# A two-layer decode step: one more V tile kept in SBUF, a smaller ring for wo and w1, and wo in products of 512 columns

## The chip, the cores and the metric

The kernel runs on 1 core of one Trainium2 chip. The metric is the device time of one execution in microseconds (us); less is better. Times are the median of several executions, and one more execution was profiled.

## The reference

Two equal layers, with the same weights and caches, run on one token for each of 8 batches. Each layer adds attention over a cache of 4096 positions, and then a dense block:

```python
x = x + _A_ref(_layernorm(x), k_cache, v_cache, wq, wo)   # 32 query heads, 4 K/V heads of 128
x = x + _B_ref(_layernorm(x), w1, b1, w2, b2)             # gelu(x @ w1 + b1) @ w2 + b2
...
x: 8 x 1 x 1024     k, v: 8 x 4 x 4096 x 128     wq: 1024 x 4096     wo: 4096 x 1024
w1: 1024 x 3584     w2: 3584 x 1024
```

All of it is float32. One layer reads 8 MB of K and 8 MB of V for each batch, 16 MB each of wq and wo, and 14 MB each of w1 and w2, unless something is still in SBUF.

## The kernel before

**Arena.** Nearly all of SBUF is one tile, `arena`: 52 places of 0.5 MB (1024 columns of 128 partitions, `SCW`). A list written ahead of time, `stream`, names every tile that is to be loaded, its size in places and the place where it goes, in the order in which it will be used. `pump()` issues the list in order from SyncE (L244); SyncE stands at a transfer until its places have been freed, and everything behind it on the list stands too. `release()` frees a tile's places when its last product has been issued and pumps again. There is no other order of loads.

**Attention.** For each batch there are eight K tiles and eight V tiles of 1 MB, taken in transfers of 1, 2 or 4 MB (the lists in `batch(...)` give size in places and place). `scores()` (L557) multiplies K, `probs()` does the softmax, `values()` (L600) multiplies V, `heads()` (L612) folds the result into `oT`. Layer 0 takes the batches from 0 to 7, layer 1 from 7 to 0, so that tiles of batch 7's V that are still in SBUF need not be loaded again: `n_kept` of them, 7.

**wo, w1.** `project()` (L383) multiplies `oT` by wo: for each of 32 heads, four products of 256 columns, one to each quarter of the output's partitions, all added up in one PSUM tile `y`. L392 adds `y` to the residual. `layernorm()` follows, then `expand()` multiplies w1 (L273; the last group of columns in L276), and each group of 512 columns goes through `hidden()`: a scaled copy on ScalarE (L290), transposes (L356), and the gelu on DVE (L360 to L373). In layer 0, while 7 MB of kept V (places 28 to 41) and 14 MB of wq (places 0 to 27) stay where they are, wo and w1 go through a ring: places 42, 45, 48, 50, of 3, 3, 2 and 2 places, so tiles of 1.5 and 1 MB.

**w2 and the next layer's queries.** `swap()` runs between the layers. In each of eight steps it multiplies 128 columns of w2 (L421, `down`), adds the result to the transposed residual `xv` (L485), and at once multiplies that part of `xv` by its rows of wq (L319, `q_part`), in two halves: `used(k, 0)` right then, `used(k, 1)` deferred to the next step. Each half frees its places of wq, and w2's later parts go there: `W2_PARTS` and `W2_LAST` name the places. w2 stays for layer 1, where `down_row()` (L439) multiplies it in the other direction, four blocks after each group of w1. A pair of w2 blocks is one product of 256 columns where the two lie next to each other or at a distance that is a power of two, otherwise two products of 128 columns. The last rows of w2 are loaded again at the very end (`LATE`).

**Small things.** `bsel` is a matrix that adds up the four quarters of the partitions; `row_s` is a scratch row of 512 columns.

Of the kernel before, what the change touches and what calls it, by code (L numbers as in the profile page):

```python
# [8 lines left out]
F32 = mybir.dt.float32  # L9
# [34 lines left out]
W2_PARTS = (((0, 16, 42), (16, 8, 44)), ((0, 16, 46), (16, 8, 48)), ((16, 8, 49), (0, 16, 50)), ((16, 8, 45), (0, 16, 2)),  # L44
            ((0, 16, 4), (16, 8, 6)), ((0, 16, 8), (16, 8, 10)), ((16, 8, 7), (0, 16, 11)), ((0, 16, 13), (16, 8, 15)))
W2_LAST = 45, 0, 1, 0
W2_COLS = NFT * Q4
LATE_AT = 0, 1, 40, 41
# [61 lines left out]
def decode_layers(ctx: ExitStack, tc: tile.TileContext, x, kc, vc, wq, wo, w1, w2, out):  # L110
# [12 lines left out]
    bits = const.tile([P, 3 + B + 2 * HQ + REP + T + 18], F32, name="bits")  # L123
# [36 lines left out]
    idq = ident.rearrange("p (j r h) -> p j r h", j=HKV, r=4)[:, :, 0, :]  # L160

    bsel = bit(B)
    nc.vector.tensor_reduce(bsel, idq.rearrange("p j h -> p h j"), AX.X, ALU.add)
# [213 lines left out]
    def project(name, lhs, resid, rsum, hooks={}):  # L377
        y = ps_o.tile([P, CH], F32, tag="o", name="y")
        n = 0
        for slot in tiles((name,)):  # L380
            for c in range(0, slot.cols, D):
                for j in range(4):
                    nc.tensor.matmul(y[32 * j:32 * j + 32, 0:Q4], lhs[:, n * B:n * B + 32],  # L383
                                     slot.ap[:, c + j * Q4:c + (j + 1) * Q4],
                                     start=(n == 0), stop=(n == HQ - 1))
                n += 1
                if n in hooks:
                    hooks[n]()
            release(slot)
            flush()  # L390
        assert n == HQ
        nc.vector.scalar_tensor_tensor(resid, y[:, 0:Q4], 1.0, resid, op0=ALU.mult, op1=ALU.add, accum_out=rsum)  # L392
# [54 lines left out]
    def swap():  # L447
# [15 lines left out]
        for s in range(NT):  # L463
# [23 lines left out]
            if k < NT - 1:  # L487
                used(k, 0)
                late.append(lambda k=k: used(k, 1))
# [223 lines left out]
    n_kept = 7  # L713
# [25 lines left out]
    batch(0, last_b, ((8, 28), (4, 36), (4, 40)), ((2, 48), (8, 28), (4, 36), (2, 40)))  # L739
    weights(("o0",), wo[0], [3, 3, 2, 2] * 3 + [2], fixed(*(42, 45, 48, 50) * 3, 42))  # L740
    weights(("i0",), w1[0], [1, 3, 2, 2] + [3, 3, 2, 2] * 2, fixed(44, 45, 48, 50, *(42, 45, 48, 50) * 2))
# [8 lines left out]
    batch(1, last_b, ((2, 16), (4, 20), (4, 24), (2, 18), (2, 0), (2, 16)), ((2, 20),))  # L750
    batch(1, last_b - 1, ((4, 24), (2, 22), (4, 16), (2, 0), (4, 36)), ((8, 28), (8, 16)))
# [129 lines left out]
```

## Time and profile before

| | us |
|---|---|
| median of 3 runs | 851.18 (850.93 to 853.94) |
| profiled execution | 850.72 |
| its span, first to last instruction | 848.9 |
| TensorE (PE) busy | 527.5 |
| VectorE (DVE) busy | 203.3 |
| ScalarE (ACT) busy | 56.4 |
| HBM read | 357.78 MB |

The span is what the profile's views count in; 1.8 us of the execution lie around it. Times in the views are us from the span's start. The layers' parts lie about so: queries of layer 0 until 48, attention until 361, wo until 398, w1 until 433, swap until 477, attention of layer 1 until 775, wo until 806, w1 and w2 until 846.

### The profile page before, as it was taken

What the parts mean: (1) busy time and instruction counts of PE and PEld (TensorE: products, weight loads), DVE (VectorE), ACT (ScalarE), POOL (GpSimd) and SP (SyncE); (2) the same over time, 40 slices, a digit from 0 to 9 for tenths busy, and PEclk for the clock granted to TensorE, in tenths of its full rate; (3) what the DMA queues carried; (4) which work ended last, traced back from release to release, by engine and by line L of the source; (5) the groups of instructions that cost most, each with busy time, mean ns of one, the idle gap of its engine ahead of it and who ended that gap; (6) DMA issues with size and microseconds to landing.
All of it is one profiled execution on the core that took longest, in us unless ns stands there. A gap on an engine that the chain in (4) does not pass through costs nothing.

```text
span 848.9 us, 9798 instructions
## 1 busy us (share of the span) xinstructions
PE 527.5 (62%) x4234; PEld 178.4 (21%) x4234; DVE 203.3 (24%) x698; ACT 56.4 (7%) x120; POOL 2.2 (0%) x13
## 2 busy tenths in 40 slices
PE   0745655566656657556778785576655666555787
PEld 0211111111111111122234222121111121112345
DVE  0013232313223131400121243141413222231022
ACT  0110000000000000000211100000000000000031
POOL 0000000000000000000000000000000000000000
PEclk9987868767787878787899988877878786888779
DMA  9999999999999999999999999999999999999997
GB/s 401 419 430 436 422 437 422 439 425 435 422 427 439 424 434 429 418 423 416 414 408 416 422 395 433 432 440 424 435 429 432 428 434 430 432 431 432 419 424 285
DMA packets 22362, 358.53 MB, mean 422 GB/s; under 512 B 2480, under 2 KB 3120, under 8 KB 5424
## 3 DMA queue, kind: packets, MB, share of 16 engines
q1 hardware_dynamic: 22176, 357.77, 99.1%
q8 instruction: 33, 0.54, 0.3%
q10 hardware_dynamic: 144, 0.15, 0.1%
q14 instruction: 9, 0.07, 0.0%
HBM read 357.78 MB, written 0.13 MB: 422 GB/s over the span
## 4 chain that ended last, share of the span: by engine, by line
DMA 73%; PE 22%; DVE 2%; issue 1%; another core or an unknown queue 1%; ACT 1%; SPq 0%; ACTq 0%; DVEq 0%
DMA arena<-in_k_dram 26%; DMA arena<-in_v_dram 22%; DMA arena<-in_w_dram 12%; PE o_ps L600 8%; DMA arena<-in_wo_dram 8%; PE sps L557 7%; DMA arena<-in_wq_dram 5%; PE y L383 1%; PE acc L273 1%; PE acc L319 1%; PE sps L421 1%; PE sps L612 1%; PE sps L590 0%; ACT sps L581 0%
## 5 line engine op out<-in xcount | busy, mean ns | idle before, releaser
L557 PE MATMUL sps<-arena,qz 128*32 128x512 f32 x1024 | 166.1, 793 | 118.3 <-DMA arena<-in_k_dram 117.8
L600 PE MATMUL o_ps<-arena 128*32 128x512 f32 x512 | 86.0, 802 | 52.4 <-DMA arena<-in_v_dram 45.5
L600 PE MATMUL o_ps<-arena,spare 128*32 128x512 f32 x512 | 81.0, 749 | 40.9 <-DMA arena<-in_v_dram 31.7
L557 PEld LDWEIGHTS sps<-arena,qz 128*32 128x32 f32 x1024 | 37.5, 135 | 211.4 <-issue 169.3
L605 DVE SCALAR_TENSOR_TENSOR scr<-o_ps,bits,scr 128x128 f32<-128x128 f32 x192 | 67.4, 351 | 6.8
L383 PE MATMUL y<-arena,oxT 128*32 128x256 f32 x512 | 42.6, 488 | 29.6 <-DMA arena<-in_wo_dram 29.6
L603 DVE TENSOR_SCALAR scr<-o_ps,bits 128x128 f32<-128x128 f32 x64 | 22.4, 351 | 144.1 <-PE o_ps L600 144.1
L273 PE MATMUL acc<-arena,oxT 128*32 128x512 f32 x192 | 33.1, 724 | 9.9 <-DMA arena<-in_w_dram 9.5
L319 PE MATMUL acc<-arena,oxT 128*32 128x512 f32 x248 | 32.4, 635 | 7.1 <-DMA arena<-in_wq_dram 4.5
L612 PEld LDWEIGHTS sps<-bits,scr 128*128 128x128 f32 x128 | 21.9, 215 | 67.4 <-issue 45.6
L600 PEld LDWEIGHTS o_ps<-arena 128*32 128x32 f32 x512 | 16.9, 133 | 85.4 <-issue 64.8
L613 DVE TENSOR_TENSOR oxT<-sps,scr 128x8 f32<-128x8 f32 x64 | 10.5, 165 | 93.4 <-PE sps L612 93.4
L562 DVE TENSOR_SCALAR_CACHE_REDUCE spare<-sps 128x512 f32<-128x512 f32 x16 | 11.1, 692 | 87.7 <-PE sps L557 87.7
L600 PEld LDWEIGHTS o_ps<-arena,spare 128*32 128x32 f32 x512 | 16.6, 126 | 69.4 <-issue 46.9
L562 DVE TENSOR_SCALAR_CACHE_REDUCE arena<-sps 128x512 f32<-128x512 f32 x16 | 11.1, 692 | 83.4 <-PE sps L557 83.4
L581 ACT ACTIVATE sps<-arena,bits 128x512 f32<-128x512 f32 x16 | 10.9, 682 | 284.2 <-DVE scr L575 284.2
L383 PEld LDWEIGHTS y<-arena,oxT 128*32 128x32 f32 x512 | 18.1, 135 | 52.3 <-DMA arena<-in_wo_dram 33.8
L581 ACT ACTIVATE sps<-spare,bits 128x512 f32<-128x512 f32 x16 | 10.9, 682 | 267.1 <-DVE scr L575 267.1
L612 PE MATMUL sps<-bits,scr 128*128 128x8 f32 x128 | 27.8, 290 | 0.0
L571 PE MATMUL sps<-scr,bits 128*128 128x128 f32 x32 | 7.6, 322 | 22.9 <-DVE scr L567 22.9
L421 PE MATMUL sps<-arena,oxT 128*32 128x128 f32 x448 | 16.0, 275 | 4.0 <-DMA arena<-in_w_dram 3.7
L204 PE MATMUL sps<-ident,xb 128*128 128x128 f32 x6 | 1.5, 344 | 24.3 <-DMA xb<-in_x_dram 23.2
(125 smaller groups left out, 256.2 us busy)
## 6 DMA issues: line engine op xcount, KB each, us to landing
arena<-in_v_dram SPq DMA_DIRECT2D x26, 4096.0 KB, 21.7
arena<-in_k_dram SPq DMA_DIRECT2D x21, 4096.0 KB, 21.5
arena<-in_k_dram SPq DMA_DIRECT2D x19, 2048.0 KB, 17.3
arena<-in_w_dram SPq DMA_DIRECT2D x16, 1024.0 KB, 10.4
arena<-in_v_dram SPq DMA_DIRECT2D x7, 2048.0 KB, 18.7
arena<-in_wo_dram SPq DMA_DIRECT2D x3, 4096.0 KB, 23.6
arena<-in_w_dram SPq DMA_DIRECT2D x6, 2048.0 KB, 23.1
arena<-in_wo_dram SPq DMA_DIRECT2D x6, 1536.0 KB, 10.5
```

The lines of the kernel that those rows point to most:

```text
L273: nc.tensor.matmul(acc[32 * j:32 * j + 32, :], lhs, slot.ap[:, c:c + CH], start=(kt < 4), stop=(kt >= NT - 4))
L319: nc.tensor.matmul(acc[u][32 * j:32 * j + 32, d0 - j * CH:d1 - j * CH], xnT[:, kt * XS:kt * XS + 32], ap[:, d0 - c0:d1 - c0], start=(kt == ...
L383: nc.tensor.matmul(y[32 * j:32 * j + 32, 0:Q4], lhs[:, n * B:n * B + 32], slot.ap[:, c + j * Q4:c + (j + 1) * Q4], start=(n == 0), stop=(n ...
L421: nc.tensor.matmul(y[32 * g:32 * g + 32], h_at(kt), arena.ap[:, a:a + P], start=(n < 4), stop=(n >= NFT - 4))
L557: nc.tensor.matmul(ps[32 * g:32 * g + 32, :], qz[:, c:c + 32], kt[:, g * CH:(g + 1) * CH], start=(j == 0), stop=(j == HKV - 1))
L562: nc.vector.tensor_scalar(st["row", b].ap[:, half * CH:(half + 1) * CH], ps, SCALE, None, op0=ALU.mult, op1=ALU.max, accum_out=st["mx", b] ...
L581: nc.scalar.activation(pp, row[:, h * CH:(h + 1) * CH], AF.Exp, bias=bias, scale=1.0, accum_out=ls[:, h:h + 1])
L600: nc.tensor.matmul(o[32 * g:32 * g + 32, :], s[:, g], v[:, g * CH:(g + 1) * CH], start=(half == 0), stop=(half == NH - 1))
L603: nc.vector.tensor_scalar(r, o[:, 0:P], sel_t[:, 0:1], None, op0=ALU.mult)
L605: nc.vector.scalar_tensor_tensor(r, o[:, t * P:(t + 1) * P], sel_t[:, t:t + 1], r, op0=ALU.mult, op1=ALU.add)
L612: nc.tensor.matmul(po[:, 0:REP], r_s[j % 2], sel_h, start=True, stop=True)
L613: nc.vector.tensor_tensor(oT_v[:, j * REP:(j + 1) * REP, b], po[:, 0:REP], rl_s[b % 2][:, j * REP:(j + 1) * REP], ALU.mult)
```

## The change

Seven edits go together:

- `n_kept` is 8: all of batch 7's V stays for layer 1, which loads none of it.
- The ring of layer 0's wo and w1 is four tiles of 1 MB, in places 44, 46, 48 and 50 (eight places in all).
- `W2_PARTS`, `W2_LAST` and `LATE_AT` name other places for w2; batches 7, 6 and 5 of layer 1 get other places and cuts.
- `project()` multiplies wo in two products of 512 columns for each head. Even heads go to quarters 0 and 2 of the output's partitions, odd heads to quarters 1 and 3.
- So `y` holds two halves for each column that have to be added: DVE copies one half of the partitions to `row_s`, ScalarE the other, and four products with `fold`, a matrix of 32 columns that takes the place of `bsel` and contains it, add them up.
- In `swap()`, the first step multiplies its second half of wq at once.
- `bits` grows by 24 columns for `fold`.

```diff
-W2_PARTS = (((0, 16, 42), (16, 8, 44)), ((0, 16, 46), (16, 8, 48)), ((16, 8, 49), (0, 16, 50)), ((16, 8, 45), (0, 16, 2)),
-            ((0, 16, 4), (16, 8, 6)), ((0, 16, 8), (16, 8, 10)), ((16, 8, 7), (0, 16, 11)), ((0, 16, 13), (16, 8, 15)))
-W2_LAST = 45, 0, 1, 0
+W2_PARTS = (((0, 16, 44), (16, 8, 50)), ((0, 16, 48), (16, 8, 46)), ((16, 8, 47), (0, 16, 0)), ((16, 8, 51), (0, 16, 4)),
+            ((16, 8, 3), (0, 16, 6)), ((0, 16, 10), (16, 8, 9)), ((0, 16, 12), (16, 8, 2)), ((0, 16, 14), (16, 8, 8)))
+W2_LAST = 51, 2, 8, 16
...
-LATE_AT = 0, 1, 40, 41
+LATE_AT = 40, 41, 42, 43
...
+    fold = bit(32)
+    nc.vector.tensor_reduce(fold, ident.rearrange("p (j m) -> p m j", j=4), AX.X, ALU.add)
+    bsel = fold[:, 0:B]
...
-                for j in range(4):
-                    nc.tensor.matmul(y[32 * j:32 * j + 32, 0:Q4], lhs[:, n * B:n * B + 32],
-                                     slot.ap[:, c + j * Q4:c + (j + 1) * Q4],
-                                     start=(n == 0), stop=(n == HQ - 1))
+                for h in range(2):
+                    g = 2 * h + n % 2
+                    nc.tensor.matmul(y[32 * g:32 * g + 32, :], lhs[:, n * B:n * B + 32],
+                                     slot.ap[:, c + h * CH:c + (h + 1) * CH], start=(n < 2), stop=(n >= HQ - 2))
...
-        nc.vector.scalar_tensor_tensor(resid, y[:, 0:Q4], 1.0, resid, op0=ALU.mult, op1=ALU.add, accum_out=rsum)
+        nc.vector.tensor_copy(row_s[0:P // 2], y[0:P // 2])
+        nc.scalar.activation(row_s[P // 2:P], y[P // 2:P], AF.Copy)
+        both = small_ps("s")
+        for j in range(4):
+            at = slice(j // 2 * 64, j // 2 * 64 + 64)
+            nc.tensor.matmul(both[32 * j:32 * j + 32, 0:Q4], fold[at], row_s[at, j % 2 * Q4:(j % 2 + 1) * Q4], start=True, stop=True)
+        nc.vector.scalar_tensor_tensor(resid, both[:, 0:Q4], 1.0, resid, op0=ALU.mult, op1=ALU.add, accum_out=rsum)
...
-                late.append(lambda k=k: used(k, 1))
+                if s == 0:
+                    used(k, 1)
+                else:
+                    late.append(lambda k=k: used(k, 1))
...
-    n_kept = 7
+    n_kept = 8
...
-    batch(0, last_b, ((8, 28), (4, 36), (4, 40)), ((2, 48), (8, 28), (4, 36), (2, 40)))
-    weights(("o0",), wo[0], [3, 3, 2, 2] * 3 + [2], fixed(*(42, 45, 48, 50) * 3, 42))
-    weights(("i0",), w1[0], [1, 3, 2, 2] + [3, 3, 2, 2] * 2, fixed(44, 45, 48, 50, *(42, 45, 48, 50) * 2))
+    batch(0, last_b, ((8, 28), (4, 36), (4, 40)), ((4, 28), (8, 32), (4, 40)))
+    weights(("o0",), wo[0], [2] * 16, fixed(*(48, 46, 44, 50) * 4))
+    weights(("i0",), w1[0], [2] * 14, fixed(*(48, 46, 44, 50) * 4))
...
-    batch(1, last_b, ((2, 16), (4, 20), (4, 24), (2, 18), (2, 0), (2, 16)), ((2, 20),))
-    batch(1, last_b - 1, ((4, 24), (2, 22), (4, 16), (2, 0), (4, 36)), ((8, 28), (8, 16)))
-    batch(1, last_b - 2, ((4, 36), (4, 24), (8, 28)), ((8, 16), (8, 24)))
+    batch(1, last_b, ((2, 20), (2, 22), (4, 24), (4, 16), (2, 20), (2, 22)), ())
+    batch(1, last_b - 1, ((4, 24), (4, 16), (4, 20), (4, 28)), ((8, 32), (8, 16)))
+    batch(1, last_b - 2, ((4, 24), (4, 28), (8, 32)), ((8, 16), (8, 24)))
```

What the numbers in the lists move shows in the order of the instructions. On SyncE, through wo, w1 and the first of w2, the list of transfers was this (128x2048 is 1 MB, 128x3072 1.5 MB, 128x1024 0.5 MB; `in_w_dram` is w1 and then w2):

```order
L244 DMA arena<-in_wo_dram 128x3072 x2
L244 DMA arena<-in_wo_dram 128x2048 x2
L244 DMA arena<-in_wo_dram 128x3072 x2
L244 DMA arena<-in_wo_dram 128x2048 x2
L244 DMA arena<-in_wo_dram 128x3072 x2
L244 DMA arena<-in_wo_dram 128x2048 x3
L244 DMA arena<-in_w_dram 128x1024
L244 DMA arena<-in_w_dram 128x3072
L244 DMA arena<-in_w_dram 128x2048 x2
```

The same list with the change, as far as the first part of w2 that goes into place 0 (the last row):

```order
L244 DMA arena<-in_wo_dram 128x2048 x16
L244 DMA arena<-in_w_dram 128x2048 x15
L244 DMA arena<-in_w_dram 128x1024 x2
L244 DMA arena<-in_w_dram 128x2048
L244 DMA arena<-in_w_dram 128x1024 x2
L244 DMA arena<-in_w_dram 128x2048
```

wo's 13 transfers are 16 equal ones; the row of 15 is w1's 14 and the first of w2, and 4 MB of w2 stand ahead of the part for place 0.

On TensorE, at the end of layer 1 before the change, wo (L383) goes over into the layer norm, w1 (L273) and the first group of w2 (L439):

```order
L383 MATMUL y<-arena,oxT 32x256 x112
L204 MATMUL sps<-ident,xb 128x128 x2
L206 MATMUL sps<-bits 128x8
L195 MATMUL sps<-bits 32x1 x8
L273 MATMUL acc<-arena,oxT 32x512 x8
L356 MATMUL sps<-ident,scr 128x128 x4
L273 MATMUL acc<-arena,oxT 32x512 x8
L439 MATMUL sps<-arena,oxT 32x256
L439 MATMUL sps<-arena,oxT 32x128 x2
L439 MATMUL sps<-arena,oxT 32x256 x3
```

The same place with the change, where wo is L385 and w2 is L446:

```order
L385 MATMUL y<-arena,oxT 32x512 x56
L398 MATMUL sps<-scr,bits 32x256 x4
L204 MATMUL sps<-ident,xb 128x128 x2
L206 MATMUL sps<-bits 128x8
L195 MATMUL sps<-bits 32x1 x8
L273 MATMUL acc<-arena,oxT 32x512 x8
L356 MATMUL sps<-ident,scr 128x128 x4
L273 MATMUL acc<-arena,oxT 32x512 x8
L446 MATMUL sps<-arena,oxT 32x256 x16
```

wo has half the products, the four of L398 stand between it and the layer norm, and the group of w2 is 16 products of one size. The last two of w2's six groups have become, with the change (the fifth group shown from its start):

```order
L446 MATMUL sps<-arena,oxT 32x128 x2
L446 MATMUL sps<-arena,oxT 32x256
L446 MATMUL sps<-arena,oxT 32x128 x6
L446 MATMUL sps<-arena,oxT 32x256
L446 MATMUL sps<-arena,oxT 32x128 x6
```

Here three of four pairs lie at distances that need two products of 128 columns; before, it was one of four pairs in every group.

## Rows read from the trace of the kernel before

**Rows 1.** The page: busy time and instructions, DMA tenths, instruction queue, chain.

```profile
PE 527.5 (62%) x4234; PEld 178.4 (21%) x4234; DVE 203.3 (24%) x698; ACT 56.4 (7%) x120; POOL 2.2 (0%) x13
...
DMA  9999999999999999999999999999999999999997
...
q8 instruction: 33, 0.54, 0.3%
...
DMA 73%; PE 22%; DVE 2%; issue 1%; another core or an unknown queue 1%; ACT 1%; SPq 0%; ACTq 0%; DVEq 0%
```

**Rows 2.** Timeline of layer 0's wo: start, us, engine, line, names, [idle before].

```profile
367.11 1.07 PE L383 MATMUL y<-arena,oxT 128*32 128x256 f32 x16 [0.53 <-DMA arena<-in_wo_dram]
369.59 1.07 PE L383 MATMUL y<-arena,oxT 128*32 128x256 f32 x16 [1.41 <-DMA arena<-in_wo_dram]
...
373.27 2.23 PE L383 MATMUL y<-arena,oxT 128*32 128x256 f32 x24 [2.62 <-DMA arena<-in_wo_dram]
```

**Rows 3.** Timeline of TensorE, w1 and w2 of layer 1.

```profile
809.69 3.64 PE L273 MATMUL acc<-arena,oxT 128*32 128x512 f32 x16 [1.11 <-DMA arena<-in_w_dram]
...
820.59 1.93 PE L273 MATMUL acc<-arena,oxT 128*32 128x512 f32 x16
...
829.27 1.92 PE L273 MATMUL acc<-arena,oxT 128*32 128x512 f32 x16 [0.20 <-DMA arena<-in_w_dram]
831.01 1.95 PE L439 MATMUL sps<-arena,oxT 128*32 128x256 f32 x40
...
834.18 1.92 PE L273 MATMUL acc<-arena,oxT 128*32 128x512 f32 x16 [0.63 <-DMA arena<-in_w_dram]
...
839.71 1.08 PE L276 MATMUL acc<-arena,oxT 128*32 128x128 f32 x32 [0.25 <-DMA arena<-in_w_dram]
```

**Rows 4.** Timeline of TensorE, two K tiles of layer 0's batch 7.

```profile
326.78 1.93 PE L557 MATMUL sps<-arena,qz 128*32 128x512 f32 x8 [2.69 <-DMA arena<-in_k_dram]
...
332.94 1.50 PE L557 MATMUL sps<-arena,qz 128*32 128x512 f32 x12 [0.73 <-DMA arena<-in_k_dram]
```

**Rows 5.** Windows (busy, clock, DMA share, GB/s); SyncE's issue at 502.88, and to landing.

```profile
502.00:505.00 3.00, 3.00 (x30) 0.97 (x26) 2.24 (x8) 0.00 (x0) 0.00 (x0) 1.00 0.71 229
...
502.88 0.33 SPq L244 DMA_DIRECT2D arena<-in_k_dram  x1
...
arena<-in_k_dram SPq DMA_DIRECT2D x1, 2048.0 KB, 8.3
```

**Rows 6.** The page's DMA issues: count, KB each, median us to landing.

```profile
arena<-in_wo_dram SPq DMA_DIRECT2D x6, 1536.0 KB, 10.5
...
arena<-in_w_dram SPq DMA_DIRECT2D x5, 1536.0 KB, 9.5
```

**Rows 7.** Timeline at the seam from wo to w1 in layer 0.

```profile
397.92 0.42 DVE L392 SCALAR_TENSOR_TENSOR xb<-y,xb 128x256 f32<-128x256 f32 x1 [32.14 <-PE y L383]
...
399.53 1.05 PE L273 MATMUL acc<-arena,oxT 128*32 128x512 f32 x4 [0.39 <-PE sps L195]
...
401.74 1.93 PE L273 MATMUL acc<-arena,oxT 128*32 128x512 f32 x8 [1.15 <-DMA arena<-in_w_dram]
```

**Rows 8.** SyncE's issue at 439.08, w2 into place 0, and its time to landing.

```profile
439.08 0.33 SPq L244 DMA_DIRECT2D arena<-in_w_dram  x1
...
arena<-in_w_dram SPq DMA_DIRECT2D x1, 512.0 KB, 6.1
```

**Rows 9.** Prices: a group of the page, then timeline rows of L421 and L383.

```profile
L562 DVE TENSOR_SCALAR_CACHE_REDUCE spare<-sps 128x512 f32<-128x512 f32 x16 | 11.1, 692 | 87.7 <-PE sps L557 87.7
...
440.20 0.86 PE L421 MATMUL sps<-arena,oxT 128*32 128x128 f32 x24 [0.18 <-DMA arena<-in_w_dram]
...
364.62 0.64 PE L383 MATMUL y<-arena,oxT 128*32 128x256 f32 x8 [2.09 <-DMA arena<-in_wo_dram]
```

More of the change, by code (lines that the diff above doesn't have):

```diff
@@ L122, in decode_layers @@
     make_identity(nc, ident)
-    bits = const.tile([P, 3 + B + 2 * HQ + REP + T + 18], F32, name="bits")
+    bits = const.tile([P, 3 + 32 + 2 * HQ + REP + T + 18], F32, name="bits")
     used = [0]
@@ L159, in decode_layers @@
     oT_v = oT[:, 0:HQ * B].rearrange("p (h b) -> p h b", b=B)
-    idq = ident.rearrange("p (j r h) -> p j r h", j=HKV, r=4)[:, :, 0, :]
-    bsel = bit(B)
-    nc.vector.tensor_reduce(bsel, idq.rearrange("p j h -> p h j"), AX.X, ALU.add)
+    fold = bit(32)
+    nc.vector.tensor_reduce(fold, ident.rearrange("p (j m) -> p m j", j=4), AX.X, ALU.add)
+    bsel = fold[:, 0:B]
     neg_m = bit(HQ)
```

## The prediction

> **What bounds the kernel now.** I read the page first. TensorE is busy 62% of the span, while the 16 DMA engines stand at nine tenths in all but the last slice, and 73% of the chain that ended last is DMA [rows 1]. So I ask of every edit what it does to one thing, the stream of transfers that SyncE issues in order, and only then what TensorE adds behind it. The timeline of TensorE shows the stream's pace, since TensorE waits for each tile as it lands: 367.11 to 369.59 is 2.48 us for a tile of 1 MB, 369.59 to 373.27 is 3.68 us for one of 1.5 MB [rows 2]; 829.27 to 834.18 is 4.91 us for 2 MB [rows 3]. A tile costs its bytes, and almost nothing for being a tile of its own: 1.5 times 2.48 is 3.72, against 3.68.
>
> Then I looked for where the stream falls behind this pace. Two causes show. First, instruction loads: the page counts 33 of them, 0.54 MB, 16 KB each [rows 1]. One fell among the K tiles that TensorE waited for at 326.78 and 332.94: 6.16 us for 2 MB instead of 4.91, 1.25 us more [rows 4]. Second, one real gap: from 502 to 505 us the DMA share is 0.71, so the engines stood still for 0.29 x 3 = 0.87 us on the mean [rows 5]. The K tile issued at 502.88 came too late: it landed after 8.3 us, of which 4.9 are its own bytes. So an issue that has only about 3.4 us ahead of its own bytes is the edge at which the queue runs dry; I use that below. Elsewhere the engines are busy to nine tenths or more [rows 1], and no edit on TensorE alone can gain there.
>
> The profiled execution took 850.72 us (span 848.9), 0.46 under the median of 851.18; I make the sum against 850.72 and let the forecast stand for the median too, since 0.46 is far inside the range.
>
> **The change, part by part.**
>
> *One V tile less.* All eight V tiles of batch 7 stay, so layer 1 doesn't load the 1 MB of its first: -2.48 us, on the path, because the stream is the path.
>
> *Other cuts.* wo and w1 of layer 0 were 11 tiles of 1.5 MB [rows 6], 13 of 1 MB and one of 0.5 MB; they become 30 of 1 MB: 30 x 2.48 = 74.4 against 11 x 3.68 + 13 x 2.48 + 1.24 = 74.0, so +0.4. Two pairs of 1 MB tiles (V of batch 7, K of batch 6) become one tile of 2 MB each: 2 x (4.91 - 4.96), -0.1. The list of transfers grows from 154 to 156. Stream in all: **-2.2**.
>
> A page of the Trainium skill speaks against smaller cuts: "DMA: Bandwidth & Descriptors", section "Anatomy of one DMA", fits about 2.0 us fixed for each DMA (of another issue path than SyncE's) beside its bytes. If that were paid in line, two more transfers would cost 4 us by an estimate from it and the stream's -2.2 would be +1.8. The trace disagrees for queued transfers: 1 MB tiles land 2.48 us apart [rows 2].
>
> *The ring.* It shrinks from five MB to four places of 1 MB. A place is issued again once its tile is multiplied, about 1.1 us after landing (the groups of rows 2 take 1.07). Three other tiles, 7.4 us, stand ahead then, and 7.4 - 1.1 = 6.3 us is well over 3.4. Cost 0; this cover goes only where TensorE pauses. At the first wo/w1 seam it pauses for the layer norm, 1.6 us from L392's addition at 397.92 to the first product of w1 at 399.53 [rows 7], and by the 1.4 below; 6.3 - 1.6 - 1.4 leaves 3.3, on the edge. I take 0, bound 0 to 0.87.
>
> *w2 in other places.* Through the ring went 10 half-MB units of w2 before the first that needs a place freed by the swap's own products; now 8. That first transfer was issued at 439.08 and landed 6.1 us later, 1.24 of it its own, so 4.8 ahead [rows 8]. Being 1 MB earlier in the stream takes 2.5 of it: 2.3, below the edge. Against this, the second query half of the first step is multiplied at once instead of one step later, which frees the next place sooner. Bounds 0 to 0.87 (one gap like rows 5).
>
> *The gap at 502.* It was a K tile of batch 6 for places 36 to 39, which held kept V until the end of batch 7. Now these K tiles go to 16 to 31, and only 28 to 31 hold V, its first two tiles. The gap should go: -0.87 to 0 (0 if the engine that is furthest behind did not stand still in it). With the risk at w2 I take **-0.5** for both, nearer the removed gap, since that one was seen and the other is argued.
>
> *wo in products of 512 columns.* 4 products of 256 columns per head become 2 of 512, so per MB the same columns: 16 records took 1.07 us there, and the 16 records of 512 for 2 MB at 820.59 took 1.93 [rows 2, 3]. No time, but 128 products fewer in both layers together; eight come in at the ends and none of w2's are lost. A product is two matmul records and two weight loads; 120 x 4 = 480 instructions at 8468 / 33 = 257 a load is two loads fewer. -1.25 to 0; each load is one packet [rows 1], so it sits on one DMA engine of 16, and a load saved on an engine that isn't last gives nothing: I take 0.
>
> *The new end of project().* DVE copies half of y (nearest: L562, 128x512 from PSUM, 692 ns), ScalarE the other half beside it, four products of 256 columns add the halves (nearest: eight records of L383, 0.64 us) [rows 9], plus a hop of 0.05 for each: 1.4 us more before L392's addition, twice. In layer 0 TensorE then waits 1.15 us for w1 anyway, at 401.74 [rows 7], and the ring covers the rest: 0. In layer 1 it waits 1.11 us before the first w1 tile at 809.69 [rows 3], so 0.3 is left over. The later tiles find TensorE waiting 0.20, 0.63 and 0.25 us; that absorbs it, unless something adds to it.
>
> *w2's pairs.* What adds to it: in layer 1 a group of four blocks was 12 products of 256 and 8 of 128 columns, 1.95 us [rows 3]. Now the first four groups are 16 of 256, the last two 4 of 256 and 24 of 128. A record of 128 columns takes 0.86 / 24 = 36 ns [rows 9], one of 256 some 60: 48 x 36 + 8 x 60 = 2.21 us, +0.26 in each of the last two, where only 0.25 of slack is left.
>
> The tail is thus 0 at best. At worst one more w1 tile runs at the lower clock, 3.64 instead of 1.93 us (809.69 and 820.59, the levels 1.2 and 2.4 GHz): 0.3 + 0.5 + 1.7 - 1.1 of slack = 1.4. I take **+0.4**.
>
> Sum: -2.2 - 0.5 + 0.4 = -2.3, **848.4 us**.
>
> **Rivals.**
>
> *A, the stream gains more.* The gap goes whole and one instruction load's worth with it, the tail costs nothing: -2.2 - 0.9 - 1.25 = -4.3, 846.4. For it: 33 loads at up to 1.25 us are the largest loss in the stream. Against: the 0 argued above.
>
> *B, given back.* w2 opens a gap of its own in place of the old one and the tail pays 1.4: -2.2 + 0 + 1.4 = -0.8, 849.9; with a second gap 850.8. For it: 2.3 us ahead at the first swap place, and 0.25 us of slack in the tail.
>
> *C, slower: the swap starves the queue.* Each of seven swap steps frees places only after its own w2 has landed. If every issue stays under 3.4 us ahead, each step adds a gap: 7 x 0.87 = 6.1, and the tail's worst 1.4: -2.2 + 6.1 + 1.4 = +5.3, 856.0. It decides once the ring can't refill between steps; at 4.8 ahead before, 2.5 less, this isn't excluded, but TensorE is faster per step than the stream, so it should recover.
>
> *D, each transfer pays for its start.* By the 3.4 us of rows 5, two more transfers: -2.2 + 6.8 + 0.4 = +5.0, 855.7. The skill's page named above stands behind it. Against: the 2.48 us of rows 2.
>
> **How the numbers follow.** Forecast 0.56, A 0.15, B 0.23, C 0.05, D 0.01. About 0.5%, 4.3 us, is what a measurement of this kernel can tell from no change: 846.9 and 855.4 are the lines. A lies below 846.9 in two thirds of its cases, so faster 0.10; C and D give slower 0.06; the rest, 0.84, is the same. The range takes in most of A and B: 846.4 to 851.0.
>
> **What would show it.** In the changed profile HBM read is 1 MB less; wo tiles land 2.48 us apart; the DMA share near 500 us is 1.0; 31 instruction loads; the first w1 product of layer 1 starts late by some 0.3 us against its tile, and TensorE waits again by the fourth. I am wrong in the stream if the share falls below 0.9 between 435 and 475 us (B or C), and in the tail if from the last w2 tile's landing to the end takes over 0.5 us more than before.

## The result, and the profile after

The changed kernel took 855.7 us (median of 17 runs, 853.2 to 861.29), the old one 851.89 beside it (17 runs, 850.11 to 855.36): ratio 1.0045, 95% interval 1.0033 to 1.0058, so 3.8 us slower. The forecast was 848.4, its range 846.4 to 851.0. The profiled execution took 861.29 us, the longest of the 17, so its losses are larger than the median's (10.6 us against 3.8); run e2 below, profiled at 854.97, shows their usual size.

The page of the changed kernel, the lines of [rows 1] and the sum of what was read:

```profile
PE 538.1 (63%) x3994; PEld 170.1 (20%) x3994; DVE 204.8 (24%) x700; ACT 57.6 (7%) x122; POOL 2.2 (0%) x13
...
DMA  9999999999999999999988999999999999999996
...
q8 instruction: 31, 0.51, 0.2%
...
HBM read 356.73 MB, written 0.13 MB: 415 GB/s over the span
...
DMA 70%; PE 26%; DVE 2%; issue 1%; ACT 1%; another core or an unknown queue 1%; SPq 0%; ACTq 0%; DVEq 0%
```

The read is 1 MB less and the loads are 31, both as forecast. But the DMA tenths now have two eights, and the chain is 70% DMA and 26% TensorE, 73 and 22 before. Windows over the stretches from wo to layer 1's first batches (busy times, granted clock, DMA share, GB/s), after:

```profile
356.00:398.00 42.00, 26.45 (x164) 5.06 (x160) 4.62 (x16) 0.00 (x0) 0.00 (x0) 0.81 1.00 408
398.00:416.00 18.00, 12.00 (x80) 3.53 (x80) 3.18 (x13) 5.51 (x10) 0.00 (x0) 0.72 0.90 347
436.00:480.00 44.00, 34.15 (x574) 19.56 (x578) 5.86 (x27) 3.88 (x5) 0.63 (x1) 0.88 0.88 336
480.00:500.00 20.00, 14.28 (x132) 5.11 (x124) 5.99 (x23) 2.24 (x4) 0.00 (x0) 0.91 0.99 403
500.00:512.00 12.00, 6.80 (x32) 1.58 (x28) 3.62 (x12) 1.52 (x4) 0.00 (x0) 0.58 1.02 434
```

The same windows before:

```profile
356.00:398.00 42.00, 25.96 (x290) 9.94 (x282) 3.65 (x14) 0.00 (x0) 0.00 (x0) 0.80 1.01 420
398.00:416.00 18.00, 12.31 (x73) 3.13 (x73) 2.42 (x12) 4.92 (x9) 0.00 (x0) 0.78 1.01 422
436.00:480.00 44.00, 36.41 (x578) 18.45 (x582) 8.78 (x37) 5.40 (x6) 0.63 (x1) 0.96 1.01 413
480.00:500.00 20.00, 12.96 (x94) 3.37 (x90) 6.36 (x20) 1.52 (x4) 0.00 (x0) 0.83 1.02 428
500.00:512.00 12.00, 10.47 (x94) 3.21 (x90) 4.75 (x17) 0.00 (x0) 0.00 (x0) 1.00 0.95 382
```

GB/s tells what is lost: 42 x 12/420 = 1.2 us up to 398, 18 x 75/422 = 3.2 at the seam from wo to w1, 44 x 77/413 = 8.2 in the swap, 20 x 25/428 = 1.2 behind it; won are 12 x 52/434 = 1.4 at the old gap near 502 [rows 5] and the forecast's 2.2 of bytes. In all +10.2, of 10.6 measured. It is a rough account, since the windows are cut at the same times while the changed kernel's work lies up to 10 us later.

Rows of the change carry its own line numbers: L385 is project()'s product (L383 before), L393 to L399 its new end, L428 w2's product in the swap (L421 before); L273 and L319 are as before.

**The seam**, the timeline of TensorE and of SyncE's next issue after, as [rows 7]:

```profile
399.14 1.72 PE L385 MATMUL y<-arena,oxT 128*32 128x512 f32 x8 [1.42 <-DMA arena<-in_wo_dram]
401.73 1.59 PE L398 MATMUL sps<-scr,bits 64*32 64x256 f32 x8 [0.88 <-DVE scr L393]
403.87 0.69 PE L204 MATMUL sps<-ident,xb 128*128 128x128 f32 x2 [0.54 <-DVE xb L399]
...
405.29 3.64 PE L273 MATMUL acc<-arena,oxT 128*32 128x512 f32 x16 [0.30 <-DVE oxT L208]
...
407.29 0.33 SPq L244 DMA_DIRECT2D arena<-in_w_dram  x1
```

That issue's KB and its time to landing:

```profile
arena<-in_w_dram SPq DMA_DIRECT2D x1, 1024.0 KB, 4.9
```

The last wo tile lands at 399.1, and the first place of the ring that w1 frees is issued at 407.29, 8.2 us later. Four tiles, 4 x 2.48 = 9.9 us, stood queued; 1.7 were left ahead of this issue, under the 3.4 of [rows 5], and the tile landed 4.9 us after it, 2.4 more than its bytes, so 0.7 were lost. The next tile landed 4.10 us later in place of 2.48. All of it ran at or near the lower clock, 1.2 GHz, as the windows show:

```profile
400.00:404.00 4.00, 2.59 (x14) 0.54 (x10) 1.12 (x3) 0.59 (x1) 0.00 (x0) 0.50 1.01 422
404.00:410.00 6.00, 5.70 (x44) 2.11 (x48) 0.82 (x4) 2.68 (x5) 0.00 (x0) 0.53 0.69 250
```

**The swap**, the timeline of TensorE and of one issue after:

```profile
442.92 0.42 PE L428 MATMUL sps<-arena,oxT 128*32 128x128 f32 x8 [2.14 <-DMA arena<-in_w_dram]
...
444.60 3.64 PE L319 MATMUL acc<-arena,oxT 128*32 128x512 f32 x16 [0.26 <-DVE oxT L493]
...
446.59 0.33 SPq L244 DMA_DIRECT2D arena<-in_w_dram  x1
...
448.01 2.98 PE L428 MATMUL sps<-arena,oxT 128*32 128x128 f32 x56
...
460.48 2.05 PE L428 MATMUL sps<-arena,oxT 128*32 128x128 f32 x40 [2.62 <-DMA arena<-in_w_dram]
```

The first w2 transfer into a place of wq goes out at 446.59 with 1.2 us ahead of it and again lands after 4.9 us, 2.4 beyond its bytes; in [rows 8] 4.8 us stood ahead of it. At 460.48 TensorE waits 2.62 us for a transfer that could only be issued when TensorE had freed its place: each keeps the other waiting.

**The tail** in layer 1, as [rows 3]:

```profile
820.54 3.62 PE L273 MATMUL acc<-arena,oxT 128*32 128x512 f32 x16
...
840.49 1.93 PE L273 MATMUL acc<-arena,oxT 128*32 128x512 f32 x16 [0.20 <-DMA arena<-in_w_dram]
845.41 1.92 PE L273 MATMUL acc<-arena,oxT 128*32 128x512 f32 x16 [0.68 <-DMA arena<-in_w_dram]
847.15 1.98 PE L446 MATMUL sps<-arena,oxT 128*32 128x128 f32 x56
```

It starts 0.6 us after its tile landed (0.3 forecast) and at the lower clock, and waits for tiles again from the fifth on. The fifth group of w2 takes 1.98 us, where the prediction added up 2.21. From the last w2 landing to the end it is 4.0 us in both traces: the tail costs nothing.

### The profile page after: what moved, and what is told of

It reads as the page before. It is cut to its first block, busy times and chain, and to the rows that moved or that the text cites. A ratio compares the mean times of both kernels' runs of the same rounds, so it can differ in the third digit from the quotient of the medians.

```text
span 859.5 us, 9335 instructions
## 1 busy us (share of the span) xinstructions
PE 538.1 (63%) x3994; PEld 170.1 (20%) x3994; DVE 204.8 (24%) x700; ACT 57.6 (7%) x122; POOL 2.2 (0%) x13
## 4 chain that ended last, share of the span: by engine, by line
DMA 70%; PE 26%; DVE 2%; issue 1%; ACT 1%; another core or an unknown queue 1%; SPq 0%; ACTq 0%; DVEq 0%
DMA arena<-in_k_dram 25%; DMA arena<-in_v_dram 22%; DMA arena<-in_wo_dram 9%; PE o_ps L610 9%; DMA arena<-in_w_dram 8%; PE sps L567 8%; DMA arena<-in_wq_dram 5%; PE acc L319 2%; PE y L385 1%; PE acc L273 1%; PE sps L428 1%; PE sps L622 1%; PE sps L446 1%; PE sps L600 0%
## 5 line engine op out<-in xcount | busy, mean ns | idle before, releaser
L567 PE MATMUL sps<-arena,qz 128*32 128x512 f32 x1024 | 167.9, 801 | 118.3 <-DMA arena<-in_k_dram 118.1
L385 PE MATMUL y<-arena,oxT 128*32 128x512 f32 x256 | 41.6, 765 | 32.2 <-DMA arena<-in_wo_dram 32.2
L319 PE MATMUL acc<-arena,oxT 128*32 128x512 f32 x248 | 37.0, 718 | 6.4 <-DMA arena<-in_wq_dram 3.8
L273 PE MATMUL acc<-arena,oxT 128*32 128x512 f32 x192 | 31.6, 772 | 8.1 <-DMA arena<-in_w_dram 7.8
L428 PE MATMUL sps<-arena,oxT 128*32 128x128 f32 x448 | 17.2, 299 | 7.0 <-DMA arena<-in_w_dram 6.6
L385 PEld LDWEIGHTS y<-arena,oxT 128*32 128x32 f32 x256 | 7.4, 126 | 61.9 <-DMA arena<-in_wo_dram 47.6
```

The costliest lines, as they stand in the source:

```text
L273: nc.tensor.matmul(acc[32 * j:32 * j + 32, :], lhs, slot.ap[:, c:c + CH], start=(kt < 4), stop=(kt >= NT - 4))
L319: nc.tensor.matmul(acc[u][32 * j:32 * j + 32, d0 - j * CH:d1 - j * CH], xnT[:, kt * XS:kt * XS + 32], ap[:, d0 - c0:d1 - c0], start=(kt == ...
L385: nc.tensor.matmul(y[32 * g:32 * g + 32, :], lhs[:, n * B:n * B + 32], slot.ap[:, c + h * CH:c + (h + 1) * CH], start=(n < 2), stop=(n >= ...
L428: nc.tensor.matmul(y[32 * g:32 * g + 32], h_at(kt), arena.ap[:, a:a + P], start=(n < 4), stop=(n >= NFT - 4))
L567: nc.tensor.matmul(ps[32 * g:32 * g + 32, :], qz[:, c:c + 32], kt[:, g * CH:(g + 1) * CH], start=(j == 0), stop=(j == HKV - 1))
```

## The experiments

In short, with the ratio to the old kernel and its interval:

| run | edit | ratio (interval) |
|---|---|---|
| the change | | 1.0045 (1.0033 to 1.0058) |
| e1 | change, old project() | 1.0014 (0.9998 to 1.0030) |
| e2 | change, old order in swap() | 1.0045 (1.0031 to 1.0059) |
| e3 | change, both | 1.0014 (1.0001 to 1.0028) |
| e4 | old kernel, new project() | 1.0010 (0.9993 to 1.0026) |
| e5 | change, unread products at the seam | 1.0187 (1.0162 to 1.0212) |
| e6 | change, less query work in swap() | 1.0040 (1.0026 to 1.0054) |
| e7 | old kernel, other places near 502 | 0.9987 (0.9974 to 0.9999) |
| e8 | e1, w2's shared tile in halves | 1.0006 (0.9992 to 1.0020) |
| e9 | change, unread products, spread | 1.0009 (0.9995 to 1.0023) |
| e10 | change, less query work, spread | 1.0033 (1.0016 to 1.0051) |
| e11 | e7, one V tile less at no price | 0.9969 (0.9957 to 0.9981) |
| e12 | change, w1 in 28 tiles | 1.0059 (1.0038 to 1.0079) |
| e13 | e9 with e8's halves | 1.0009 (0.9998 to 1.0021) |
| e14 | e13, old project(), more lead | 1.0017 (1.0004 to 1.0029) |
| e15 | e7, unread products | 0.9987 (0.9978 to 0.9996) |
| e16 | e15, more instruction loads | 0.9992 (0.9979 to 1.0004) |
| e17 | e13, more instruction loads | 1.0008 (0.9992 to 1.0024) |
| e18 | e15, new project() | 0.9982 (0.9970 to 0.9993) |

**One edit undone, or one alone (e1 to e4).**

```diff
e1: project() as before
e2: -                if s == 0:
    -                    used(k, 1)
    -                else:
    -                    late.append(lambda k=k: used(k, 1))
    +                late.append(lambda k=k: used(k, 1))
e3: e1 and e2
e4: the old kernel with project(), fold and bits of the change
```

> The changed kernel with the old project(): four products of 256 columns per head and no adding up of halves at its end; ring, places, kept V and swap() stay as changed. In the changed profile TensorE needs 8.2 us from the landing of the last wo tile (399.10) to the first freed place of w1 (issue 407.29), and the queue then loses about 2.3 us in two transfers (3.20 and 4.10 us in place of 2.48). Theory S (the seam: the longer end of project() on a ring 1 MB smaller): about 1.4 us of the 8.2 go, more at the lower clock, the share between 404 and 410 us goes from 0.69 to 0.95 or more, and the kernel comes 1.5 to 2.3 us nearer to the old one: 853.4 to 854.2 against 855.7, ratio 1.002 to 1.003. Theory W (the swap alone: 4 MB of w2 stand ahead of its first freed place, 5 before): no change that can be told, ratio 1.004 to 1.005, and the share from 440 to 470 stays at 0.7 to 0.9.

> The changed kernel with one edit of swap() undone: the second query half of the first step waits again for the next step's products. Theory L (the half multiplied at once holds up step 1's products by 1.1 us, 1.9 at the lower clock, and so all later places): the gaps between 446 and 470 us shrink by 1 to 2 us, ratio 1.002 to 1.003. Theory W (the queue is dry before that half is multiplied at all: the first place is issued at 446.59 with 1.2 us ahead of it): the first gap stays as it is, and the place of the second half comes free later, by step 1's products (3 us for 56 records in the changed profile), so the same or slower: ratio 1.004 to 1.008.

> The changed kernel with both undone: the old project() and the old order in swap(); what is left is the eighth kept V tile, the ring of four tiles of 1 MB and the other places. If project() and the order of the first step account for the loss, 851.9 less the 2.2 of the stream and the 0.9 of the gap at 502 is left: 848.8, ratio 0.996 to 0.998. If it is the ring and the 1 MB less of w2 ahead (theory W), the swap starves as before and the kernel stays slower than the old one: ratio 1.002 to 1.006.

> The old kernel with the new project() alone (512 columns per product, halves added up at the end, fold in place of bsel); ring of 5 MB, seven kept V tiles, old places. If the longer end hurts only where the ring can't cover it (theory S): share 0.98 or more through both seams of layer 0, and only the tail's 0 to 0.4 us of layer 1 is left, ratio 1.000 to 1.001. If the longer end costs in itself, once in each layer: 2 x 1.4 = 2.8 us, ratio 1.003.

The old project() gives back 0.0031, 2.6 us (theory S, a little over its 2.3). The order in the first step is worth nothing, with or without that (e2, e3). The new project() alone, on the ring of 5 MB, costs nothing that its interval can tell (e4). So the longer end is dear with the ring of 4 MB; that it is cheaper with 5 MB is likely, not shown, since e4's interval still allows 2.2 us. With 5 MB it runs short now and then: e4's profiled execution, 856.13 us against its median of 851.7, moved 357 GB/s from 398 to 416 us at a clock of 0.73. And e1 is still 1.2 us slower than the old kernel (its interval just takes in no difference), where bytes and gap should make it 3.1 faster: the swap loses too, as theory W has it. Windows of e2, at the ratio of the change and an ordinary time:

```profile
398.00:416.00 18.00, 12.60 (x94) 3.90 (x92) 3.38 (x14) 5.52 (x10) 0.00 (x0) 0.78 0.98 387
...
436.00:480.00 44.00, 34.10 (x599) 17.70 (x599) 7.55 (x33) 5.00 (x7) 0.63 (x1) 1.00 0.97 370
```

By the same working 1.5 us are lost at this seam and 4.6 in the swap. The DMA share of the swap is 0.97, yet 10% fewer bytes move. So the sign that the prediction named for a starved swap, a share below 0.9, shows over this stretch in the trace of the longest execution (0.88) and not in an ordinary one.

**Is it the clock? (e5, e9, e15)**

```diff
+        d = ps_o.tile([P, CH], F32, tag="o", name="d")
+        for j in range(4):      # e5: d[0:32, :] each time
+            nc.tensor.matmul(d[32 * j:32 * j + 32, :], ident[:, 0:32], spare[:, 0:CH], start=True, stop=True)
```

> The changed kernel with products added that nothing reads, to keep TensorE busy through layer 0's first seam: four of 512 columns after each of the last seven wo tiles but the last, two while y's halves are copied, two while the sum is added to the residual. Theory C (TensorE's lower clock makes the seam long: in the changed profile the granted clock is 0.50 from 400 to 408 us, the last wo tile takes 1.72 us, L398 1.59 and the first w1 records 3.64 for 16, so 8.2 us from the last wo tile's landing to the first freed place of w1): the clock stays at 1.0 through the seam, that time falls to about 6 us, the 0.6 to 2.3 us that the queue loses at 404 to 412 go, ratio 1.002 to 1.0035 against 1.0045. Theory S without the clock (the longer end of project() is too long at either clock): no gain, ratio 1.004 to 1.005. The other way is possible too: eight records more per tile delay the release of wo's places while the clock is still low, and the queue loses elsewhere before 400 us.

> The changed kernel with unread products again, this time four of 512 columns to the four groups of 32 output rows in turn: 8 records took 1.07 us in that form, where the last run's, all to one group, took 3.17 for 7 at full clock and made TensorE the bound. After the wo tiles of heads 20 to 31 but the last, while y's halves are copied, and while the sum is added. Theory C (the lower clock makes the seam long): the clock is 1.0 from the second of these tiles on, the first freed place of w1 is issued 6 us after the last wo tile's landing instead of 8.2, the queue loses under 0.5 us there, ratio 1.002 to 1.0035. Theory S without the clock: 1.004 to 1.005. If the added 1.07 us per tile hold up wo's releases: 1.005 to 1.007.

> The old kernel with the other places (0.9987) and the same unread products after wo's last tiles and beside the residual's addition. If they help only where the ring can't cover the lower clock: no change, 0.998 to 0.9995. If the lower clock costs the old kernel as well: 0.9955 to 0.997. If they delay the seam: above 0.9995.

e5 made the change slower by 1.4%, so it is no test of the clock, but it shows something else. TensorE's timeline of e5:

```profile
384.37 3.17 PE L386 MATMUL d<-spare,ident 128*32 128x512 f32 x7
```

And of e9:

```profile
397.68 1.07 PE L392 MATMUL y<-arena,oxT 128*32 128x512 f32 x8 [0.57 <-DMA arena<-in_wo_dram]
398.56 1.04 PE L386 MATMUL d<-spare,ident 128*32 128x512 f32 x8
...
402.80 1.92 PE L273 MATMUL acc<-arena,oxT 128*32 128x512 f32 x16 [0.34 <-DVE oxT L208]
```

Products that follow each other into one group of 32 output rows took 0.45 us a record, those that go round the four groups 0.13: e5 made TensorE the bound. In e9 they fit into the waits, the clock stays up, and the first freed place is issued at 403.93, 6.3 us after the last wo tile landed (6 expected). Windows of e9:

```profile
398.00:416.00 18.00, 11.83 (x111) 3.56 (x103) 3.89 (x17) 5.52 (x10) 0.00 (x0) 1.00 1.01 415
436.00:480.00 44.00, 34.24 (x604) 18.44 (x602) 8.54 (x38) 6.02 (x9) 0.63 (x1) 1.00 0.96 376
```

415 GB/s at the seam, for 347 in the change's trace and 387 in e2's, and 0.0036 or 3.1 us of time. The same products give e15 nothing (0.9987 as e7). So theory C holds: what the seam loses it loses to the lower clock, where the ring can't cover it (e15 has the old project() and the long ring; which of the two covers it there, it doesn't tell). The 17 runs of the change fit it: eight with a mean clock of 0.804 or more have a median of 854.6 us, the nine below 856.5, while the 35 of the old kernel beside e1 to e4, parted in the same way, have 851.4 on both sides. That is a hint and no more, since a mean over the whole kernel doesn't name a seam. The swap is hardly touched: 376 GB/s, for 370 in e2.

**The gap, the gift, the cuts (e7, e11, e12).**

```diff
e7: -    batch(0, last_b, ((8, 28), (4, 36), (4, 40)), ((2, 48), (8, 28), (4, 36), (2, 40)))
    +    batch(0, last_b, ((8, 28), (4, 36), (4, 40)), ((2, 48), (4, 28), (8, 32), (2, 40)))
    -    batch(1, last_b - 1, ((4, 24), (2, 22), (4, 16), (2, 0), (4, 36)), ((8, 28), (8, 16)))
    +    batch(1, last_b - 1, ((4, 24), (2, 22), (4, 16), (2, 0), (4, 28)), ((8, 32), (8, 16)))
    -    batch(1, last_b - 2, ((4, 36), (4, 24), (8, 28)), ((8, 16), (8, 24)))
    +    batch(1, last_b - 2, ((4, 24), (4, 28), (8, 32)), ((8, 16), (8, 24)))
e11: e7, V tile 1 of batch 7 multiplied in layer 1 in the place of tile 0, and
    -(2, 0), (2, 16)), ((2, 20),))
    +(2, 0), (2, 16)), ())
e12: +    weights(("i0",), w1[0], [1] * 28, fixed(*(48, 49, 46, 47, 44, 45, 50, 51) * 4))
```

> The old kernel with other places for three batches only: batch 7's V tiles 1 and 2 in places 28 to 31 and 3 to 6 in 32 to 39, the last K tile of batch 6 in 28 to 31 and its first V tile in 32 to 39, batch 5's K in 24, 28 and 32. Seven V tiles kept, ring of 5 MB, old project() and swap(). If the gap at 502 us comes from that K tile's place (36 to 39, freed only after V tile 6), it goes, and nothing else moves: 0.9 to 1.0 us less, ratio 0.9985 to 0.9995. If another transfer is late there instead, no change: 1.000.

> The old kernel with the other places of the run that removed the gap at 502 (ratio 0.9987), and one more V tile less to load at no price in room: layer 1's first V tile of batch 7 is not loaded, and the second one, which is still there, is multiplied in its place (so that tile's part of the result is left out). Ring of 5 MB, old project() and swap(). If the 1 MB is worth its 2.48 us of stream, and the changed kernel lost it to the ring that paid for it: 0.9987 - 0.0029 = 0.9958, 0.995 to 0.9965. If the transfer was hidden or its gain is given back later in layer 1: 0.998 to 0.999.

> The changed kernel with layer 0's w1 in 28 tiles of 0.5 MB in place of 14 of 1 MB, in the same eight places: 14 transfers more. At the seam the first place comes free after half a tile's products, 0.9 us sooner at full clock, 1.8 at the lower. Theory S: the loss at the seam (0.5 to 2.3 us in the runs so far) falls by 0.5 to 1.5 us; the cuts cost 14 x (2 x 1.25 - 2.48) = 0.3: ratio 1.003 to 1.0045. Rival D (every transfer pays for its own start): 14 x 2 to 3.4 = 28 to 48 us more, ratio 1.035 or above.

e7 gains 1.1 us, 0.9 to 1.0 expected, and the window of [rows 5] is full in its trace:

```profile
502.00:505.00 3.00, 3.00 (x30) 0.97 (x26) 2.24 (x8) 0.00 (x0) 0.00 (x0) 1.00 1.04 440
```

So the gap came from that place. e11 is 0.0018 or 1.5 us below e7; its ratio of 0.9969 lies just outside the range expected, but the interval takes in the 2.48 us. Against e3 it is the test of the ring: both load none of batch 7's V in layer 1, with the old project() and the old order, and differ in ring and places, which no run separates: 0.0045, 3.8 us. The swap's window of e3:

```profile
436.00:480.00 44.00, 35.22 (x599) 19.16 (x598) 7.46 (x34) 3.88 (x5) 0.63 (x1) 0.95 0.94 354
```

And of e11:

```profile
436.00:480.00 44.00, 36.45 (x590) 18.65 (x589) 9.20 (x39) 5.63 (x7) 0.63 (x1) 0.97 1.02 417
```

These two profiled executions lie 6.9 us apart (854.90 and 848.04), and 44 x 63/417 = 6.6 us of it is this window.

e12 misses: the seam gained nothing. The first freed place is issued at 408.30, 8.4 us after the last wo tile, at the lower clock, and 2.0 us after w1's first product, as with whole tiles; why the half tile's place wasn't issued sooner isn't shown. But 14 transfers more cost 1.2 us against the change, 0.1 each, where rival D has 2 to 3.4 for each. It falls. The Trainium skill ("DMA: Bandwidth & Descriptors", "Anatomy of one DMA") fits a fixed 2.0 us for each DMA, of another issue path than SyncE's, which would make 14 x 2.0 = 28 us as an estimate; this run disagrees for transfers that queue.

**What starves the swap? (e6, e10, e8, e13, e14, e16, e17)**

```diff
e6:  +            q_part(acc, u, kt, 0, slot.ap if u == 0 or kt == first else slot.ap[:, 0:CH], first)
e10: the second halves of steps 1 to 6 as four products of 128 columns
e8:  ("w2", "last", 0) as two transfers of 4 x 128 columns, the second behind step 1's blocks (on e1)
e13: e9 with e8's edit
e14: e13 on the old project(); every place of wq released by itself, W2_PARTS[2] in three parts
e16, e17: +            for _ in range(1024):
          +                nc.gpsimd.memset(dust, 0.0)
```

> The changed kernel, but the second query halves of swap()'s steps 1 to 6 multiply only one of their four pieces of 512 columns, so three quarters of that half's work are left out; places, transfers and the order stay. Theory P (TensorE sets the pace of the swap: in the old profile four steps take 438.93 to 457.56, 4.66 us each, while the stream needs 3.5 x 1.24 = 4.34 us per step, so a short lead never grows): each step is 0.78 us shorter, 3.9 us, the lead grows by 0.4 us per step, and the losses after the first two steps go: idle share from 450 to 490 us under 0.02, ratio 1.001 to 1.0025. Theory W (only the first place comes too late, the rest are instruction loads or chance): ratio 1.004 to 1.005.

> The changed kernel, but the second query halves of swap()'s steps 1 to 6 multiply only 128 of each 512 columns (three quarters of that half's work are left out), in the four groups of output rows as before. The last run's single product took 1.02 us for 2 records, as long as all 8 with 1.04, so it shortened no step; this form should take 0.3 us, a step 3.9 instead of 4.66, against 4.34 of stream. Theory P (TensorE's pace keeps the swap's lead short): the GB/s of 436 to 480 us rise from 336 to 384 in the runs so far to 400 or more, 2 to 3 us come back, ratio 1.0005 to 1.002. Theory W (the lead of the first place alone, or loads): ratio 1.0035 to 1.0045.

> The changed kernel with the old project(), as in the run before with that edit (ratio 1.0014), and with the 0.5 MB tile of w2's last rows that the first two swap steps share loaded in two halves of 0.25 MB, the second one behind the second step's blocks. So step 0 is complete 0.62 us earlier in the stream, and all that follows in the swap has 0.62 us more ahead of it. Theory P (TensorE's pace carries the lead of the first place through all steps): the losses between 440 and 490 us, about 5 us in that run's trace with the instruction loads in it, fall by 0.6 to 2 us, ratio 0.999 to 1.0007. If the lead of the first place does not matter for the later ones: 1.001 to 1.0015; if 512-byte pieces cost more in the queue than 0.62 us: above 1.0015.

> The changed kernel with the unread products of the run at 1.0009 and with w2's first tile of last rows in two halves, as in the run at 1.0006. Theory: seam and swap lose independently, the first by the clock, the second by the lead of its first freed place (2.3 us, then 2.9). With 0.6 us more lead the swap gives back 0.5 to 1.5 us: ratio 0.9990 to 1.0003, GB/s of 436 to 480 us 384 or more (376 with the unread products alone). If the swap's loss doesn't hang on that lead: 1.0005 to 1.0015.

> The same with the old project() (four products of 256 columns per head), the unread products after the same wo tiles and beside the residual's addition, and with each wq place of 0.5 MB in the swap released by itself, after two products in place of four, so that the first w2 transfer of a freed place, cut in two, is issued 0.5 us sooner again. By the same theory the lead at the first freed place is 2.3 + 0.6 + 0.5 = 3.4 us and the queue hardly runs dry: ratio 0.9975 to 0.9990, GB/s of 436 to 480 us 395 or more. If finer pieces and two more instruction loads eat that: 0.999 to 1.001.

> The old kernel with the other places and the unread products (0.9987), and with 1024 POOL instructions that set one unread column, from the start of the swap on, where POOL has nothing else to do: 1024 / 257 = 4 instruction loads more, on an engine that nobody waits for. Theory L (a load holds up one of the 16 DMA engines by about 1.1 us; with 5 to 10 us of transfers queued the others run on, and the next load falls on another engine, so that loads overlap; with a short queue all wait for the late one, and loads add up): 0 to 1.3 us more, ratio 0.9987 to 1.0003. If every load costs its 1.1 us whatever is queued: 4.4 us more, ratio 1.0035 to 1.0045.

> The changed kernel with unread products and split tile (1.0009), and with the same 1024 POOL instructions. Theory L: the loads that fall into the swap add up, 2 to 4.5 us more, ratio 1.003 to 1.006. If loads overlap here as well as in the old kernel: 0 to 1.3 us more, 1.0009 to 1.0025, and the instruction loads are not what is left of the changed kernel's loss.

e6 took nothing off a step, for the same reason as in e5: products into one group. TensorE's timeline of e6:

```profile
449.94 1.02 PE L319 MATMUL acc<-arena,oxT 128*32 128x512 f32 x2
...
451.55 1.06 PE L319 MATMUL acc<-arena,oxT 128*32 128x512 f32 x8 [0.26 <-DVE oxT L493]
```

The shortened half in e10's timeline:

```profile
468.50 0.40 PE L469 MATMUL acc<-arena,oxT 128*32 128x128 f32 x8
```

Two records in one group take as long as eight in four. The Trainium skill ("TensorEngine Tiling (Array Packing)", "Key Properties") says that different tiles of the array can multiply in parallel; these rows agree. e10 did shorten the half, to 0.40 us, and came to 1.0033 and 380 GB/s: 1 us of the 2 to 3 that theory P wanted. Its interval overlaps the change's, and theory P's range as well, so it speaks against TensorE's pace as the main thing and doesn't exclude it.

e8's 1.0006 against e1's 1.0014 looked like the lead, but the intervals overlap, and e13 (1.0009, 0.9998 to 1.0021) equals e9, with an interval that still allows the smaller gains that were expected. In e13 the first freed place goes out 0.9 us sooner than in e9, with 3.1 us ahead of it, and no gap stands there; the transfer three issues later loses 2.1 us instead. The rows of e13 for these two issues, time from issue to landing:

```profile
arena<-in_w_dram SPq DMA_DIRECT2D x1, 1024.0 KB, 5.6
...
arena<-in_w_dram SPq DMA_DIRECT2D x1, 1024.0 KB, 8.2
```

e14, with more lead again, is no better: 1.0017, clear of the 0.9975 to 0.9990 that the lead alone would give. The instruction loads were hardly tested. 1024 POOL instructions brought 8 loads of 8 KB, not 4 of 16 (the page of e17; e13 has 9 on this queue):

```profile
q14 instruction: 17, 0.14, 0.0%
```

They cost 0.4 us on the long queue and nothing on the short one, less than the intervals can tell. The queues of e17 from 430 to 480 us show why that says little:

```profile
q8 instruction: 6, 0.10, 0.8%
q14 instruction: 2, 0.02, 0.1%
```

Only two of POOL's loads fell into the swap, and they took 0.3 us each, TensorE's of 16 KB took 0.9 to 1.1. In e13's trace such a load of TensorE starts at 451.8, 2 us before the tile that lost 2.1 landed. So theory L is neither borne out nor refuted. **What stays open** is how 1 MB less of ring costs the swap some 4 us. That it's the ring and the places, and in this stretch, is shown (e3 and e11). That the gaps hang on the first place's lead, on TensorE's pace or on loads was argued: e14 is against the lead alone, e10 leaves the pace unclear, and the loads stand untested.

**A version that beats both (e18).** e15 with the new project() in both layers:

> The old kernel with the other places (0.9987), the new project() in both layers and the unread products at layer 0's seam: 240 products fewer, two instruction loads fewer, and the clock kept up where the longer end of project() stands. If the two loads saved are worth anything on a deep queue: 0.9975 to 0.9985. If loads overlap there and the longer end is covered: 0.9985 to 0.9995. If the longer end still shows at the seam or in layer 1: 1.000.

0.9982: faster than the old kernel by 1.5 us, and than the change by 5.4. It can't be told from e7 and e15, so what its two loads fewer are worth isn't shown.

## Why the prediction was wrong

- **Right.** 1 MB less read; wo tiles 2.48 us apart; 31 loads; the gap at 502 gone, worth 1.1 us (e7) for 0.87. The tail, taken at +0.4, costs 0. The stream's -2.2 is what e11 shows within its interval.
- **Wrong first: "The ring ... Cost 0 ... 3.3, on the edge. I take 0, bound 0 to 0.87."** By GB/s the seam costs 3.2 us in the change's trace and 1.5 in e2's; undoing project() gave back 2.6 (e1), the higher clock 3.1 (e9). The step that failed is the clock, which the sum had at its full level through the seam. The pause was added up as 1.1 + 1.6 + 1.4 = 4.1 us. Missing were the products of w1's first tile, after which alone its place is free (1 us for 8 records, and in the old kernel that tile had half a MB), and some waits: at full clock e9 measures 5.1 us from the landing to the first w1 product and 6.3 to the issue. But the cover was also one tile short, three tiles of 7.4 us for the four of 9.9 that stand queued, and the two errors cancel by luck: 9.9 - 6.3 = 3.6 us left for the 3.3 forecast, and at that clock the seam moves 415 GB/s. At the lower clock the change measures 8.2, and 1.7 are left. The lower clock was priced for layer 1's tail alone, where it did no harm.
- **The edge of 3.4 us was misread.** These rows of before are the issues just ahead of the K tile of [rows 5], and the second one's time to landing:

```profile
489.21 0.80 SPq L244 DMA_DIRECT2D arena<-in_k_dram  x2
...
arena<-in_k_dram SPq DMA_DIRECT2D x1, 1024.0 KB, 15.7
```

  The second went out at 489.6 and landed at 505.3, so 2.4 us stood ahead of the issue at 502.88; the other 1.0 of the 3.4 is what was lost. Nor do the runs show one sharp edge: 3.1 us ahead lost nothing in e13, 3.2 lost 1.6 at the change's seam.
- **Wrong second: "Bounds 0 to 0.87 (one gap like rows 5)" for w2, and "TensorE is faster per step than the stream, so it should recover".** The lead of 2.3 us was right at best: it was 2.3 in e1's trace, 1.3 in e9's, 1.2 in the change's. But a short lead was priced as one gap at one place, and the loss went on from 441 to 480: 3.8 us between e3 and e11. And the rows of before did not bear out the recovery. Its steps of L421, with their waits for transfers (one more is in [rows 9]):

```profile
438.93 1.08 PE L421 MATMUL sps<-arena,oxT 128*32 128x128 f32 x32
...
445.22 0.43 PE L421 MATMUL sps<-arena,oxT 128*32 128x128 f32 x8 [0.17 <-DMA arena<-in_w_dram]
...
448.97 1.30 PE L421 MATMUL sps<-arena,oxT 128*32 128x128 f32 x40 [0.38 <-DMA arena<-in_w_dram]
...
454.82 0.43 PE L421 MATMUL sps<-arena,oxT 128*32 128x128 f32 x8 [0.74 <-DMA arena<-in_w_dram]
...
457.56 1.92 PE L421 MATMUL sps<-arena,oxT 128*32 128x128 f32 x56
```

  Four steps take 4.66 us each, of which 0.37 are waits for transfers. That leaves 4.29 us of TensorE's own chain, while a step's 1.75 MB take 4.34: next to no margin to recover in. (Theory P took the 4.66 whole for TensorE's pace.) That was the argument by which rival C got 0.05. A shorter step gave back 1 us by its ratio (e10), so the pace isn't shown to be the cause, which stays open.
- **The rivals.** C was the case in kind. Its number is near by luck (856.0 forecast, 855.7 measured): its sum had no seam, put all in the swap and let the tail pay 1.4. D gave nearly the same time and is refuted by e12. The forecast of no change was made of -2.2 in bytes, which e11 bears out, and of costs that were each called covered.

## What to carry to other kernels

A buffer's size is not cover at one point but along every stretch in which places come free late: price a smaller ring by the longest time from the last landing to the first freed place, the next tile's products in it and at the lower clock, and for the whole stretch, not for one gap. Read GB/s beside the DMA share. Where TensorE waits for transfers ahead of such a seam, products that nobody reads, spread over all four output groups, can keep its clock up (e9); with the longer ring and the old project() they did nothing (e15).

## What the runs showed of the hardware

- Matmul records of 32 output rows: 8 over four groups 1.04 us, 2 in one group 1.02, at the higher clock.
- In the swap, traces with the ring of 4 MB showed DMA shares of 0.94 to 1.01 at 354 to 384 GB/s (the change's own 0.88 at 336), those with 5 MB 0.99 to 1.02 at 394 to 417.
- A 1 MB transfer with only 1.2 to 1.7 us of others ahead landed 4.9 us after its issue; on a busy queue it landed 2.48 after the one ahead.
- POOL's instructions came in loads of 8 KB, some 128 instructions each, that took 0.3 us; TensorE's in 16 KB, 0.9 to 1.1 us in e17.
